# A slice of the second layer's output weights loaded by a transfer with five outer rows

## The chip, the core and the metric

The kernel runs on one core of a Trainium2 chip. The time is the device time of one execution in microseconds (us). Before the change it is 2557.82 us, the median of three runs (2560.64, 2557.49 and 2557.82). A change of 0.2% is 5.1 us.

TensorE (PE) multiplies matrices, VectorE (DVE), ScalarE (ACT) and GpSimd (POOL) work on elements, and SyncE (SP) does nothing here but issue transfers. The transfers run on the core's 16 DMA engines.

## The reference

Two layers, each an attention block over a long cache followed by a gated feed-forward block, for two batch rows of one token each (decode):

```python
x = A_x
x = x + _A_ref(_layernorm(x), A_k_cache, A_v_cache, A_wq, A_wo)   # attention, 32 query heads on 8 kv heads
x = x + _B_ref(_layernorm(x), B_w_gate, B_w_up, B_w_down)         # (gelu(x @ gate) * (x @ up)) @ down
x = x + _A_ref(...); x = x + _B_ref(...)                          # the same weights and caches again
```

The model width is 512, the cache holds 32768 positions of 128 numbers for each of 2 x 8 (batch, kv head) pairs, and everything is float32. Keys and values are 268 MB each and are read once per layer, less the little that layer 2 finds still on the chip. After attention, the 4096 numbers of the 32 heads go through `wo` (4096 x 512, 8 MB): `o @ wo`. The change is in how a part of `wo` comes on the chip in the second layer.

## The kernel before, in words

One SBUF tensor, `mem`, has 110 units of 512 float32 columns on 128 partitions. A unit is 2 KB on each partition, 256 KB in all. Every weight and cache piece has a planned place in `mem` (the function `plan`). The list `stream` holds all transfers in the order of their use: for each layer the query weights `wq`, then for each of 16 (kv head, batch) pairs keys (`kt`) and values (`vt`) in pieces of 32 units, with `wo` put in near the end, then the feed-forward weights `gu` and `wd`. The function `pump` issues the head of this list on SP as soon as the bookkeeping shows that its place has been given back by `done`; on the chip, SP then waits in this order for the semaphore of the last reader of that place. So SP's order is fixed when the program is built, and a transfer that waits holds back all that stand behind it on SP.

`wo` is loaded in two pieces in each layer (`WO_PARTS`). In layer 2, piece 0 has 28 units, the columns of heads 4 to 31, and goes to the place `A_AT = 0`, where keys stood. It is issued behind the keys of pair 14 (of 0 to 15). Its reader is `project` (L768 to L776): 28 products of one head each with one unit of `wo`, into the PSUM tile `W`. `project` stands in TensorE's loop over the pairs as a part that runs in one turn only, at pair 15:

```python
turns = [g for g, _ in ORDERS[l][1::2]][:-1]
for g in turns:
    for t in range(REP):
        pe.matmul(W[...], heads(g)[:, t, :], w[:, REP * g + t - s, :], ...)
done(("wo", l, 0))
```

In layer 2 the heads come from the top down in groups of four, so the first four products read units 24 to 27 of the 28, the last of the piece.

The end of the program is the second layer's feed-forward block. Its last weights `wd` come in pieces of 4, 3, 4, 2 and 1 units; `down` (with `add_row`, L792) multiplies them as they land, the result goes through `desk` (L935) and the transfer `out` (L936).

The helper `Program` records all operations and works out the semaphore waits. A transfer takes a semaphore of its own until it is known to have landed, and counts 16 on it. An instruction that reads what three transfers wrote waits for three semaphores.

Of the kernel before, what the change touches and what calls it, by code (L numbers as in the profile page):

```python
# [15 lines left out]
P = 128  # L16
# [3 lines left out]
DM = 512  # L20
# [36 lines left out]

WO_PARTS = [[(0, 28), (28, 4)], [(4, 28), (0, 4)]]
WO_IN = 14

LAST_ROOM = "k", 1, *ORDER[-1], 35

# [351 lines left out]
AUX = 440  # L414


def block_kernel(nc, x, kt, vt, wq, wo, gu, wd, out):
    pr = Program(nc)
    pe, dve, act, pool, sp = pr.tensor, pr.vector, pr.scalar, pr.gpsimd, pr.sync

    def sbuf(name, cols):
        return nc.alloc_sbuf_tensor(name, [P, cols], F32).ap()

    mem = sbuf("mem", UNITS * UNIT)
# [5 lines left out]
    at = {}  # L430
# [3 lines left out]
    def take(key, n):  # L434
        o = planned[key]
        if not any(s <= o and o + n <= e for s, e in holes):
            return None
        for i, (s, e) in enumerate(holes):
            if s <= o and o + n <= e:
                holes[i:i + 1] = [(x, y) for x, y in ((s, o), (o + n, e)) if y > x]  # L440
                return o
# [14 lines left out]
    def pump():  # L456
        while stream:
            key, src, cols = stream[0]
            n = cols / UNIT
            o = take(key, n)  # L460
            if o is None:
                return
            stream.popleft()
            if key == LAST_ROOM:
                held.append(ROOM_AT)
            c = int(o * UNIT)
            at[key] = (o, n), mem[:, c:c + cols]
            plain = (key[0] in "kv" and key[4] in (0, CHUNK)
                     and rolled(key[0], key[1], ORDERS[key[1]].index(key[2:4])))
            sp.dma_start(at[key][1], src, sem=(key[0], key[4]) if plain else "any")  # L470

    def flat_of(key):
        if key not in at:
            pump()
        return at[key][1]
# [4 lines left out]
    def done(key, s=0, n=None):  # L480
        o, size = at[key][0]
        n = size if n is None else n
        if s + n == size:
            del at[key]
        give(o + s, n)
        pump()

    def flat(src, g, b, s, n):
        h, c = divmod(s, CHUNK)
        return src[b, g, h, :, c * UNIT:(c + n) * UNIT]  # L490

    def add(key, src, cols):
        stream.append((key, src, cols))
# [4 lines left out]
    def rolled(kind, l, n):  # L498
        return n in ROLLED if kind == "k" else n < len(ORDER) - 1

    def add_wo(l, i):
        s, m = WO_PARTS[l][i]
        add(("wo", l, i), wo[:, s * DM:(s + m) * DM], m * DM)

    for l in range(2):
        for i, (s, m) in enumerate(pieces(WQ_SPLIT[l])):
            add(("wq", l, i), wq[:, s * DM:(s + m) * DM], m * DM)
        for n, (g, b) in enumerate(ORDERS[l]):
            for s, m in parts("k", l, (g, b)):
                add(("k", l, g, b, s), flat(kt, g, b, s, m), m * UNIT)  # L510
            if n == WO_IN:
                add_wo(l, 0)
# [24 lines left out]
    xrows = desk[:KC * NB, :P]  # L537
    act.dma_start(xrows, x)
    pump()
    ident = cst[:, C_ID:C_ID + P]  # L540
    dve.memset(ident, 0.0)
# [351 lines left out]
    def finish(l, n, p, linv):  # L893
        g, b = ORDERS[l][n]
        values(l, n, g, b, p)
        if meets(l, n)[0]:
            leave()
        combine(linv, g, b, 128 if n == len(ORDER) - 1 else 0)
# [4 lines left out]
    for l in range(2):  # L903
        queries(l)
        stage(l, 0)
        for n, (g, b) in enumerate(ORDERS[l]):
            with pr.turn_of(l, n) if n in ROLLED else nullcontext():
                if n == WO_IN + 1:
                    pr.section("project")
                    with pr.apart_of():  # L910
                        project(l)
                if n:
                    pr.section("values")
                    finish(l, n - 1, *found)
                if n == WO_IN + 1:
                    pr.section("turn")
# [21 lines left out]
    pr.emit()  # L938


_INS = ["x", "kt", "vt", "wq", "wo", "gu", "wd"]


def groups(x):
# [3 lines left out]
def halves(gate, up):  # L948
    out = []
    for e in range(2):  # L950
        c, cols = e * DF // 2, []
        for n in FW:
            cols += [gate[:, c:c + n], up[:, c:c + n]]
            c += n
        w = np.concatenate(cols, axis=1).reshape(KC, P, -1).transpose(1, 0, 2)
        out.append(np.ascontiguousarray(w).reshape(-1))
    return np.concatenate(out)


# [25 lines left out]
```

## Time and profile before

| what | value |
|---|---|
| median of three runs | 2557.82 us (2557.49 to 2560.64) |
| the profiled execution | 2558.18 us, of which the span from the first to the last instruction is 2556.7 |
| TensorE, matmul | busy 1205.1 us (47%), mean granted clock 0.738 |
| VectorE, ScalarE, GpSimd | busy 143.6, 81.3 and 2.7 us |
| data moved by the queue of SP and ACT | 1102.92 MB in 25056 packets |
| HBM read | 1102.84 MB, 431 GB/s over the span |

The page has the share of busy time by engine, the span cut into 40 equal slices (a digit is tenths of busy time), the DMA queues, and the chain of work that ended last: it is followed back from the last instruction, at each step to what released it. `DMA mem<-in_kt` there is time in which the work waited for a transfer of keys. The view of windows gives the same for stretches that one chooses, with the mean busy share of the 16 DMA engines and the GB/s that they moved. A share over 1.00 comes from packets whose recorded times overlap a little.

### The profile page before, as it was taken

The numbers are of one execution on the slowest core, as the hardware profiler recorded it, in microseconds if no ns is written. First come the engines' busy times: TensorE is split into PE (matmuls) and PEld (weight loads), VectorE is DVE, ScalarE is ACT, GpSimd is POOL, SyncE is SP. The second block draws the span as 40 slices with busy tenths as digits, with TensorE's granted clock in tenths as the row PEclk, the third lists the DMA queues.
The fourth block names the chain that finished last, engine by engine and source line by source line (L and its number), as shares of the span: only waits on it lengthen the run. The fifth ranks groups of instructions, "written<-read, shape, count | busy, mean of one in ns | idle before, by whom it ended". The sixth has DMA issues, their size and how long they took to land.

```text
span 2556.7 us, 19577 instructions
## 1 busy us (share of the span) xinstructions
PE 1205.1 (47%) x9177; PEld 317.2 (12%) x9177; DVE 143.6 (6%) x490; ACT 81.3 (3%) x190; POOL 2.7 (0%) x9
## 2 busy tenths in 40 slices
PE   3433553434544434544686444345443355343546
PEld 1100111101111111111121111111110011010112
DVE  0000000000000000000011000000000000000001
ACT  0000000000000000000010000000000000000000
POOL 0000000000000000000000000000000000000000
PEclk8766777667777767766898777677676677677778
DMA  9999999999999999999999999999999999999999
GB/s 426 428 436 430 431 438 432 438 431 437 430 431 438 432 436 432 435 429 434 427 419 436 437 431 436 431 431 438 432 438 431 436 431 431 437 433 436 433 433 386
DMA packets 25093, 1103.21 MB, mean 431 GB/s; under 512 B 2792, under 2 KB 2928, under 8 KB 5616
## 3 DMA queue, kind: packets, MB, share of 16 engines
q1 hardware_dynamic: 25056, 1102.92, 99.9%
q8 instruction: 14, 0.23, 0.0%
q14 instruction: 7, 0.06, 0.0%
q10 hardware_dynamic: 16, 0.00, 0.0%
HBM read 1102.84 MB, written 0.07 MB: 431 GB/s over the span
## 4 chain that ended last, share of the span: by engine, by line
DMA 75%; PE 23%; SPq 1%; another core or an unknown queue 0%; DVE 0%; issue 0%; ACT 0%
DMA mem<-in_kt 36%; DMA mem<-in_vt 36%; PE S L683 12%; PE A L751 11%; DMA mem<-in_wd 1%; SPq L470 1%; DMA mem<-in_gu 1%; DMA mem<-in_wq 1%; PE M L644 0%; PE A L683 0%; PE W L792 0%; ACT T L720 0%; DVE desk L722 0%; DVE aux L686 0%
## 5 line engine op out<-in xcount | busy, mean ns | idle before, releaser
L683 PE MATMUL S<-mem,aux 128*32 128x512 f32 x4032 | 543.4, 699 | 402.5 <-DMA mem<-in_kt 402.5
L751 PE MATMUL A<-mem 128*16 128x512 f32 x2048 | 292.0, 733 | 746.4 <-DMA mem<-in_vt 745.7
L683 PEld LDWEIGHTS S<-mem,aux 128*32 128x32 f32 x4032 | 137.9, 126 | 786.9 <-DMA mem<-in_kt 428.0
L751 PE MATMUL A<-mem,desk 128*16 128x512 f32 x2048 | 229.5, 601 | 12.6 <-DMA mem<-in_vt 12.6
L751 PEld LDWEIGHTS A<-mem 128*16 128x16 f32 x2048 | 61.3, 113 | 951.8 <-DMA mem<-in_vt 752.8
L686 DVE TENSOR_REDUCE aux<-S 128x1 f32<-128x512 f32 x63 | 43.6, 692 | 918.5 <-PE S L683 918.5
L766 DVE TENSOR_REDUCE aux<-M 128x4 f32<-128x64 f32 x32 | 7.2, 226 | 1334.5 <-PE M L763 1334.5
L751 PEld LDWEIGHTS A<-mem,desk 128*16 128x16 f32 x2048 | 55.3, 98 | 180.0 <-issue 167.2
L720 ACT ACTIVATE T<-S,aux 128x512 f32<-128x512 f32 x63 | 41.4, 657 | 1013.2 <-DVE aux L716 1013.2
L759 ACT ACTIVATE desk<-A,aux 128x512 f32<-128x512 f32 (+1 forms) x34 | 22.3, 662 | 1345.8 <-PE A L751 1345.8
L726 PE MATMUL M<-aux 128*128 128x4 f32 x64 | 14.6, 298 | 85.2 <-DVE aux L724 85.2
L763 PE MATMUL M<-aux,desk 128*128 128x128 f32 x128 | 21.3, 287 | 24.9 <-ACT desk L759 24.9
L644 PE MATMUL M<-mem,aux 128*32 128x512 f32 x128 | 21.2, 691 | 20.7 <-DMA mem<-in_wq 20.7
L713 PE MATMUL M<-aux 128*128 128x128 f32 x32 | 10.3, 323 | 34.5 <-DVE aux L711 34.5
L722 DVE STREAM_TRANSPOSE desk<-T 128x512 f32<-128x512 f32 x32 | 22.9, 717 | 27.0 <-ACT T L720 27.0
L726 PEld LDWEIGHTS M<-aux 128*128 128x128 f32 x64 | 11.7, 230 | 91.3 <-DVE aux L724 91.3
L722 DVE STREAM_TRANSPOSE mem<-T 128x512 f32<-128x512 f32 x32 | 22.9, 717 | 0.0
L774 PE MATMUL W<-mem,aux 128*2 128x512 f32 x112 | 17.7, 802 | 5.2 <-DMA mem<-in_wo 5.2
L763 PEld LDWEIGHTS M<-aux,desk 128*128 128x128 f32 x128 | 13.4, 141 | 53.2 <-ACT desk L759 53.2
L720 ACT ACTIVATION_READ_ACCUMULATOR T<-S,aux 128x1 f32 x63 | 12.4, 196 | 0.0
L611 PE MATMUL A<-aux 128*128 128x256 f32 (+2 forms) x38 | 12.1, 400 | 0.3 <-DVE aux L623 0.3
L713 PEld LDWEIGHTS M<-aux 128*128 128x128 f32 x32 | 4.3, 133 | 63.7 <-DVE aux L711 63.7
(108 smaller groups left out, 168.8 us busy)
## 6 DMA issues: line engine op xcount, KB each, us to landing
mem<-in_wo SPq DMA_DIRECT2D x2, 7168.0 KB
mem<-in_kt SPq DMA_DIRECT2D x2, 4096.0 KB, 16.5
mem<-in_vt SPq DMA_DIRECT2D x1, 6144.0 KB, 29.3
mem<-in_gu SPq DMA_DIRECT2D x6, 896.0 KB, 28.3
mem<-in_gu SPq DMA_DIRECT2D x3, 1792.0 KB, 40.2
mem<-in_kt SPq DMA_DIRECT2D x1, 4864.0 KB, 16.9
mem<-in_vt SPq DMA_DIRECT2D x1, 4096.0 KB, 23.8
mem<-in_vt SPq DMA_DIRECT2D x2, 2048.0 KB, 29.8
```

What stands on the lines that cost most here:

```text
L470: sp.dma_start(at[key][1], src, sem=(key[0], key[4]) if plain else "any")
L644: pe.matmul(qp[32 * t:32 * t + 32, :], window(k, v), w[:, i - s, :], start=(i < 4), stop=(i >= 8 * KC - 4))
L683: pe.matmul(banks[u][32 * t:32 * t + 32, :], pad[:, PAD_Q - 4 * c:PAD_Q + 32 - 4 * c], w[:, j - s, :], start=(j == tile_of[0]), stop=(j == ...
L686: dve.tensor_reduce(mx[:, u:u + 1], banks[u], axis=AX.X, op=OP.max)
L713: pe.transpose(m[:, :P], nm.to_broadcast([P, P]), ident)
L720: act.activation(T[u], banks[u], AF.Exp, bias=bias, scale=SCALE, accum_out=ls[:, u:u + 1])
L722: dve.transpose(p[u], T[u])
L726: pe.matmul(m[:, :REP], both.to_broadcast([P, P]), same, start=True, stop=True)
L751: pe.matmul(A[32 * t:32 * t + 16, :], p[u][:, at_p:at_p + 16], w[:, QUAD * i + t, :], start=(j == order[0]), stop=(j == order[-1]))
L759: act.activation(desk[:, i:i + 512 // n], A[:, i:i + 512 // n], AF.Copy, scale=linv)
L763: pe.transpose(m[:, c * P:(c + 1) * P], desk[:, c * P:(c + 1) * P], ident)
L774: pe.matmul(W[32 * t:32 * t + NB, :], heads(g)[:, t, :], w[:, REP * g + t - s, :], start=(g == turns[0]), stop=(g == turns[-1]))
```

## The change

The host makes a second copy of a part of `wo`, the array `wn`: of the last 768 columns of piece 0 (1.5 units, 3072 bytes on a partition) the rows of partitions 0 to 124, as five blocks of 25 rows, each with one row of zeros behind it. The zeros keep the five blocks apart in memory, so that the source of a transfer of 5 x 25 rows has an outer dimension of five. Where `pump` comes to piece 0 of layer 2, it now issues three transfers in place of one: 26.5 units on 128 partitions as before, the 1.5 units of 125 partitions from `wn`, and those of the last 3 partitions from `wo`. The place in `mem`, the readers and the order of all else are as they were. Layer 1 is not changed. The same bytes are moved.

```diff
 WO_IN = 14
+
+LANES = 5
+EACH = P // LANES
+SLIM = 768
+SLIM_AT = WO_PARTS[1][0][0] * DM + WO_PARTS[1][0][1] * DM - SLIM
...
-            sp.dma_start(at[key][1], src, sem=(key[0], key[4]) if plain else "any")
+            if key == ("wo", 1, 0):
+                slim = mem[:, c + cols - SLIM:c + cols]
+                sp.dma_start(mem[:, c:c + cols - SLIM], src[:, :cols - SLIM])
+                sp.dma_start(slim[:LANES * EACH], wn[:, :EACH])
+                sp.dma_start(slim[LANES * EACH:], src[LANES * EACH:, cols - SLIM:])
+            else:
+                sp.dma_start(at[key][1], src, sem=(key[0], key[4]) if plain else "any")
...
+def lanes(wo):
+    w = wo[:LANES * EACH, SLIM_AT:SLIM_AT + SLIM].reshape(LANES, EACH, SLIM)
+    return np.concatenate([w, np.zeros_like(w[:, :1])], axis=1)
...
+    arrays["wn"] = lanes(arrays["wo"])
```

In the built program, these rows stand on SP near the end of layer 2. A row is a line, an operation, what it writes and reads, the written shape, and the semaphores it waits for (`s_6` counts TensorE's finished instructions). Before:

```order
L470 DMA mem<-in_kt 128x16384
L470 DMA mem<-in_kt 128x16384 [waits s_6]
L470 DMA mem<-in_wo 128x14336 [waits s_6]
L470 DMA mem<-in_vt 128x16384
L470 DMA mem<-in_vt 128x16384 [waits s_6]
```

After the change, at the same place:

```order
L481 DMA mem<-in_kt 128x16384
L481 DMA mem<-in_kt 128x16384 [waits s_6]
L477 DMA mem<-in_wo 128x13568 [waits s_6]
L478 DMA mem<-in_wn 125x1x768 [waits s_6]
L479 DMA mem<-in_wo 3x768
L481 DMA mem<-in_vt 128x16384
L481 DMA mem<-in_vt 128x16384 [waits s_6]
```

Two transfers are added on SP, between the long one and the values of pair 14; the second of the three has a wait of its own, since the long one no longer covers the last 1.5 units of the old keys.

On TensorE, `project` in layer 2 is the only place that reads the piece. Before:

```order
L351 COMPARE_AND_BRANCH
L774 MATMUL W<-mem,aux 2x512 [waits s_0]
L774 MATMUL W<-mem,aux 2x512 x27
L351 UNCONDITIONAL_BRANCH
L751 MATMUL A<-mem 16x512 [waits s_9]
```

After the change:

```order
L356 COMPARE_AND_BRANCH
L785 MATMUL W<-mem,aux 2x512 [waits s_0]
L785 MATMUL W<-mem,aux 2x512
L785 MATMUL W<-mem,aux 2x512 [waits s_2,s_1]
L785 MATMUL W<-mem,aux 2x512 x25
L356 UNCONDITIONAL_BRANCH
L762 MATMUL A<-mem 16x512 [waits s_9]
```

The first product waits for the long transfer as before; the third, the first to read the last 1.5 units, waits for the two new ones.

More of the change, by code (lines that the diff above doesn't have):

```diff
@@ L414, with block_kernel @@
 AUX = 440
-def block_kernel(nc, x, kt, vt, wq, wo, gu, wd, out):
+def block_kernel(nc, x, kt, vt, wq, wo, wn, gu, wd, out):
     pr = Program(nc)
@@ L938, in block_kernel @@
     pr.emit()
-_INS = ["x", "kt", "vt", "wq", "wo", "gu", "wd"]
+_INS = ["x", "kt", "vt", "wq", "wo", "wn", "gu", "wd"]
 def groups(x):
```

## The prediction

> **What bounds the kernel now.** I read the page's slices first, then its chain of waits, then the end of the program in the views of the chain and of windows. From the page:
>
> ```profile
> span 2556.7 us, 19577 instructions
> DMA  9999999999999999999999999999999999999999
> DMA packets 25093, 1103.21 MB, mean 431 GB/s; under 512 B 2792, under 2 KB 2928, under 8 KB 5616
> q1 hardware_dynamic: 25056, 1102.92, 99.9%
> q8 instruction: 14, 0.23, 0.0%
> q14 instruction: 7, 0.06, 0.0%
> DMA 75%; PE 23%; SPq 1%; another core or an unknown queue 0%; DVE 0%; issue 0%; ACT 0%
> ```
>
> All 16 DMA engines are busy in every slice; the packets' time fills 99.9% of the span. TensorE waits for data. So the kernel is as long as its transfers, and the change moves no byte less: it can only pay in how the 16 engines share the bytes. One engine moves 431 / 16 = 26.9 GB/s. The rows q8 and q14 count 21 transfers of instructions, about 16 KB (0.23 MB / 14) and 9 KB each. They go through the same engines, in the way of the data, and nothing says that they fall evenly.
>
> Whether the engines end together is seen only where the queue runs out. The chain at the end, and stretches of half a microsecond there (columns: stretch, length, busy time and count of PE, PEld, DVE, ACT and POOL, granted clock, DMA share, GB/s):
>
> ```profile
> 2523.43 30.22 DMA mem<-in_wd
> 2553.65 0.04 issue
> 2553.69 0.62 PE W L792 x16
> 2554.31 0.02 issue
> 2554.33 0.45 PE W L792 x8
> 2554.77 0.02 issue
> 2554.80 0.29 DVE desk L935
> ```
>
> ```profile
> 2546.00:2550.00 4.00, 3.01 (x21) 0.68 (x19) 1.56 (x4) 1.46 (x3) 0.00 (x0) 1.00 1.00 412
> 2550.00:2550.50 0.50, 0.43 (x6) 0.27 (x10) 0.01 (x1) 0.00 (x0) 0.00 (x0) 1.00 0.97 389
> 2550.50:2551.00 0.50, 0.50 (x24) 0.47 (x27) 0.18 (x1) 0.00 (x0) 0.00 (x0) 1.00 0.67 270
> 2551.00:2551.50 0.50, 0.50 (x28) 0.40 (x16) 0.00 (x0) 0.00 (x0) 0.00 (x0) 1.00 0.52 209
> 2551.50:2552.00 0.50, 0.21 (x8) 0.00 (x0) 0.00 (x0) 0.00 (x0) 0.00 (x0) 1.00 0.59 217
> 2552.00:2552.50 0.50, 0.00 (x0) 0.00 (x1) 0.00 (x0) 0.00 (x0) 0.00 (x0) 1.00 0.36 143
> 2552.50:2553.00 0.50, 0.47 (x20) 0.48 (x24) 0.00 (x0) 0.00 (x0) 0.00 (x0) 1.00 0.27 102
> 2553.00:2553.50 0.50, 0.50 (x24) 0.28 (x12) 0.00 (x0) 0.00 (x0) 0.00 (x0) 1.00 0.12 45
> 2553.50:2554.00 0.50, 0.39 (x16) 0.30 (x16) 0.00 (x0) 0.00 (x0) 0.00 (x0) 1.00 0.03 12
> ```
>
> The last piece of `wd` lands at 2553.65, and from there a fixed tail of 3 us runs to the end. But the engines do not stop together. With 412 GB/s in the last full stretch, the rows of these small pieces go at 412 / 16 = 25.8 GB/s an engine. By that, 15 engines' worth of bytes move in the first half microsecond, then 10, 8, 8, 6, 4, 2, and at the end less than one. Six engines are done by about 2550.5, eight by 2551, and the last works alone until 2553.6. This bounds all that any sharing can give: from 2550 on, half the sum of the eight last rates (1387), 694 KB, is still to come; 16 engines together need 694 / 412 = 1.7 us for it and would end at 2551.7. That is 2.0 us sooner, or 0.08%. Calling 0.2% (5.1 us) what a measurement of this kernel can tell from no change, no gain of this change can be told.
>
> **The change part by part.** The long transfer of `wo` loses 1.5 units: 128 rows of 3072 bytes, 393,216 bytes, or 24,576 on each of 16 engines. At 26.9 GB/s each engine is free 0.91 us sooner.
>
> The added transfer brings 125 rows, 384,000 bytes. If its outer dimension of five means that five engines share it, each gets 25 rows, 76,800 bytes: 2.85 us at 26.9 GB/s, 2.98 at the rate of small rows. The last three rows, if on three engines, are 3072 bytes and 0.11 to 0.12 us each. Net: eleven engines are 0.91 us earlier from here to the end, two are 1.94 to 2.07 later, three 2.05 to 2.19 later.
>
> [...]
>
> The end is the last engine's end, so the sum depends on which engines the five are. If they are among the six that are done by 2550.5, they now end at 2552.6 to 2552.7, and the slowest, no longer loaded with its share, at 2553.65 - 0.91 = 2552.74: the landing is 0.9 us earlier. If the slowest is among the five, it lands at up to 2553.65 + 2.19, which is 2.2 us later. These are the bounds, -0.9 and +2.2. No row names an engine, so this is a choice: 21 instruction transfers are too few to fall evenly on 16 engines, and where one recurring cause spares six or eight of them, these are likelier neighbours (the low numbers or the high) than six picked at random. I take -0.9, by this little better than even.
>
> Issuing. Two more transfers on SP. The rows of SP around the place (start, length, what; a long one contains its waits), and the chain there:
>
> ```profile
> 2362.71 0.33 SPq L470 DMA_DIRECT2D mem<-in_kt  x1
> 2381.37 0.33 SPq L470 DMA_DIRECT2D mem<-in_wo  x1
> 2381.74 21.12 SPq L470 DMA_DIRECT2D mem<-in_vt  x2
> ```
>
> ```profile
> 2362.71 30.00 DMA mem<-in_kt
> 2392.71 0.04 issue
> ```
>
> An issue takes 0.33 us, so the two cost 0.7, perhaps twice that for the odd shape. When `wo` is issued, at 2381.37, the keys issued ahead of it are still in flight until 2392.71: 11.3 us of queued work hide this. Uncovered it would be 0.7 us on every engine. The new wait on SP, for the keys' last products, holds back the three rows and two transfers of values behind it. Those products end at about the time of the issue (the keys' readers released SP for `wo`); of the values, the first was issued at 2381.74 and the second waits 21 us anyway. Cost: nothing.
>
> TensorE. Rows around the only reader of the piece:
>
> ```profile
> 2409.69 8.90 PE L774 MATMUL W<-mem,aux 128*2 128x512 f32 x56 [2.57 <-DMA mem<-in_wo]
> 2448.39 9.19 PE L751 MATMUL A<-mem 128*16 128x512 f32 x64 [29.80 <-DMA mem<-in_vt]
> ```
>
> It already waits 2.57 us for `wo`. Later it waits 29.80 us for values. If the five make `wo` land up to 2.2 us later, this idle time takes it, and a second semaphore wait there. Behind the waiting product stand the rest of `project` and then the products with values that are not there yet, so nobody else is late. Without that cover it would be the 2.2 us once. From here on, five engines run some 3 us behind the other eleven (2.1 + 0.9). A transfer counts as landed with its last engine; the spread at the end is already about 3 us (2550.5 to 2553.6), and of the early six the five only catch up with the slow ones. So later landings do not come later. The last piece of `wd` is on its way from 2523.43, 30.22 us before it lands, so the queue holds work for engines that run ahead.
>
> Sum: 2558.18 us of the profiled execution, less 0.9 by the landing, nothing elsewhere: 2557.3. The profiled one stands 0.36 above the median of the three runs (2557.82), so 2556.9 against the median.
>
> **The rivals.**
>
> Late engines among the five. [...] Against it nothing but the grouping argument; for it, ten of 16 are not among the early six. The landing comes 1 to 2.2 us later: an engine that ends at 2552.7 goes to 2554.8, the slowest to 2555.8. Time 2559 to 2560.
>
> [...]
> [...]
>
> The transfer narrows to fewer engines: slower. If the shapes of 5 x 25 and 125 have the whole transfer put on one engine, this one has 384,000 / 26.9 = 14.3 us in place of 0.9. From 2550.5 it ends at 2563.9, the landing is 10.2 us later, and the time 2568: slower by 0.4%. It decides from two engines down: two have 7.1 us each and end at 2556.7, 3.1 us late; from one, it is over the 0.2%. The same sign would come from rows cut into many small packets. For it: nothing in the trace; against: two ordinary sizes that have five in common.
>
> It does not do what it says: all 16 engines share the 1.5 units as before. Then the skew stays and so does the time, 2557.8.
>
> **How the numbers follow.** Five early engines 0.55 (2556.9). Late engines among the five 0.22 (2559 to 2560). Ports 0.10 (2558.8). No narrowing 0.05 (2557.8). Fewer engines or small packets 0.05 (2561 to 2568). Some gain that I don't see 0.03. The four first are all inside 5.1 us of the median before: 0.92 for no difference, of which 0.01 goes to scatter of the measurement, since the three runs alone lie 3.2 us apart. Slower 0.06, faster 0.03. For the range, the first case has the scatter of the runs (-0.3 to +2.8) on it: 2556.6 to 2559.7; less another 1.6 below for a gain at the bound of 2.0 with the scatter, and above up to the second case's 2560.6: 2555.0 to 2560.6. Below and above, 2 in 10 are left.
>
> **What would show it.** The page's packets: the 125 + 3 rows of 3072 bytes add 128 to "under 8 KB" if rows stay whole, and the endings of a transfer on five and one on three engines add 8 to "under 512 B" (32 if both run on all 16; many thousands if rows are cut up). In the windows of the last 4 us, the steps tell the case. Right: 14 to 16 engines' worth longer, no stretch with one or two engines alone, and a last landing 0.9 us earlier against the end of the span. Late engines among the five: a longer stretch of four engines or fewer. [...] One engine: 10 us with 26 GB/s. At the place itself, `project` has its wait for `wo` split in two, with the sum within 2.2 us of 2.57, and the wait for values after it is shorter by what this is longer. Wrong would be any change outside the last 5 us that moves the end: a stretch of the 40 slices under 9 tenths that is at 9 now, or a later time of the last issue on SP.

## The result, and the profile after

The change makes the kernel slower: 2563.44 us, the median of 14 runs (2563.19 to 2564.16), against 2557.93 before (14 runs, 2557.49 to 2560.64). The ratio is 1.0021, with a 95% interval of 1.0013 to 1.0029. That is 5.5 us more where 0.9 us less was forecast, and outside the range.

The page's rates before (GB/s in each of the 40 slices), and then the page of the kernel after:

```profile
GB/s 426 428 436 430 431 438 432 438 431 437 430 431 438 432 436 432 435 429 434 427 419 436 437 431 436 431 431 438 432 438 431 436 431 431 437 433 436 433 433 386
```

```profile
span 2562.4 us, 19580 instructions
DMA  9999999999999999999999999999999999999998
GB/s 425 427 437 431 437 431 437 431 437 431 436 431 437 431 437 429 439 432 434 421 424 436 432 436 431 435 433 433 435 431 436 429 436 432 435 432 435 412 435 368
DMA packets 25229, 1103.21 MB, mean 431 GB/s; under 512 B 2800, under 2 KB 2936, under 8 KB 5752
```

The same bytes move and the DMA engines look as busy as before, but the third of the 40 slices from the end moves 412 GB/s where its neighbours have 435, and where the kernel before has 433. The transfer that was changed is in it. The packets answer how it was made: 8 more under 512 bytes (2800 for 2792), the endings of a transfer on five engines and of one on three, where the trace has 16 landings for a transfer of 128 rows; and 136 more under 8 KB (5752 for 5616), these 8 and the 125 + 3 rows. The semaphore events in the trace agree: the engines land the 125 rows in five steps, at 2410.00, 2410.09, 2410.44, 2411.65 and 2415.63, and the 3 rows in three, at 2410.31, 2410.40 and 2411.85. So five engines it was, with whole rows. One of them lands 4 us behind the rest, and it is none of the three that also carried a last row, which had all landed by 2411.85.

The view of windows around that transfer (columns: stretch, length, busy time and count of PE, PEld, DVE, ACT, POOL, granted clock, DMA share, GB/s), before:

```profile
2390.00:2402.00 12.00, 9.24 (x64) 2.35 (x64) 0.00 (x0) 0.00 (x0) 0.00 (x0) 0.66 1.03 444
2402.00:2416.00 14.00, 7.69 (x47) 1.82 (x43) 3.04 (x11) 1.45 (x4) 0.00 (x0) 0.63 1.00 434
2416.00:2428.00 12.00, 2.59 (x28) 0.38 (x16) 0.00 (x0) 0.00 (x0) 0.00 (x0) 0.75 1.01 437
```

and after:

```profile
2390.00:2402.00 12.00, 9.39 (x64) 2.35 (x64) 0.00 (x0) 0.00 (x0) 0.00 (x0) 0.67 0.99 430
2402.00:2416.00 14.00, 3.47 (x15) 0.84 (x15) 3.04 (x11) 1.45 (x4) 0.00 (x0) 0.60 1.01 339
2416.00:2428.00 12.00, 7.24 (x52) 1.28 (x44) 0.00 (x0) 0.00 (x0) 0.00 (x0) 0.78 1.00 431
```

In the 14 us from 2402 to 2416, the engines are as busy as ever (share 1.01) and move 339 GB/s in place of 434. A busy share says that packets are under way, not that they go at their rate. What is missing is (434 - 339) x 14 us = 1.33 MB, which is 3.1 us of all 16 engines at 431 GB/s. This is new: the forecast only shifted bytes from engine to engine. The trace also has each packet, that is, each row of a transfer on one engine. A row of 64 KB takes 2.42 us in the kernel before; here rows of that size take up to 4.10 us. All packets of this place together take 50 us longer than packets of their sizes do undisturbed, which again is 3.1 us for each of 16 engines.

TensorE around the reader of the piece, and SP at the issue:

```profile
2410.85 1.88 PE L785 MATMUL W<-mem,aux 128*2 128x512 f32 x4 [3.84 <-DMA mem<-in_wo]
2415.67 7.57 PE L785 MATMUL W<-mem,aux 128*2 128x512 f32 x52 [2.95 <-DMA mem<-in_wn]
2454.13 9.69 PE L762 MATMUL A<-mem 128*16 128x512 f32 x64 [30.89 <-DMA mem<-in_vt]
```

```profile
2381.30 0.33 SPq L477 DMA_DIRECT2D mem<-in_wo  x1
2381.67 0.94 SPq L478 DMA_DIRECT2D mem<-in_wn  x1
2382.66 0.43 SPq L479 DMA_DIRECT2D mem<-in_wo  x1
```

The wait for `wo` is 3.84 + 2.95 = 6.8 us (2.57 before). The values that TensorE waits for next land at 2454.13, where they landed at 2448.39: 5.7 us later, and this stays to the end.

The end in the chain and in windows of the kernel after:

```profile
2527.96 31.43 DMA mem<-in_wd
2559.39 0.04 issue
2559.44 0.62 PE W L803 x16
```

```profile
2552.00:2554.00 2.00, 2.00 (x19) 0.64 (x18) 0.00 (x0) 0.13 (x1) 0.00 (x0) 1.00 0.83 336
2554.00:2556.00 2.00, 1.08 (x10) 0.12 (x7) 1.30 (x4) 1.12 (x3) 0.00 (x0) 1.00 0.39 155
2556.00:2558.00 2.00, 1.64 (x42) 1.14 (x42) 0.44 (x2) 0.22 (x1) 0.00 (x0) 1.00 0.08 31
2558.00:2559.50 1.50, 1.12 (x36) 0.83 (x40) 0.00 (x0) 0.00 (x0) 0.00 (x0) 1.00 0.10 36
```

SP at the last loads, before and after:

```profile
2498.54 32.57 SPq L470 DMA_DIRECT2D mem<-in_wd  x5
```

```profile
2504.77 31.02 SPq L481 DMA_DIRECT2D mem<-in_wd  x5
```

The last landing is at 2559.39 (2553.65 before), and SP ends the issue of the last load at 2535.79 (2531.11). From 2556 on, 31 to 36 GB/s are little more than one engine. By the semaphore events, the last but one of the 16 engines lands the last piece at 2556.22, so one works alone for 3.2 us (0.7 before: 2552.99 to 2553.65). The others are later too: half of them have landed it by 2554.65, where it was 2551.43. Two losses show, then: one engine that is later than all, and a stretch in which all are slower. The experiments part them.

### The profile page after: what moved, and what is told of

Read it like the earlier page. It is cut to its first block, busy times and chain, and to the rows that moved or that the text cites. A ratio compares the mean times of both kernels' runs of the same rounds, so it can differ in the third digit from the quotient of the medians.

```text
span 2562.4 us, 19580 instructions
## 1 busy us (share of the span) xinstructions
PE 1209.0 (47%) x9177; PEld 330.6 (13%) x9177; DVE 143.6 (6%) x490; ACT 81.3 (3%) x190; POOL 2.7 (0%) x9
## 2 busy tenths in 40 slices
DMA packets 25229, 1103.21 MB, mean 431 GB/s; under 512 B 2800, under 2 KB 2936, under 8 KB 5752
## 4 chain that ended last, share of the span: by engine, by line
DMA 73%; PE 23%; another core or an unknown queue 2%; SPq 1%; DVE 0%; issue 0%; ACT 0%
DMA mem<-in_kt 37%; DMA mem<-in_vt 33%; PE S L694 12%; PE A L762 11%; DMA mem<-in_wd 2%; DMA mem<-in_wn 1%; SPq L481 1%; DMA mem<-in_gu 1%; DMA mem<-in_wq 1%; PE W L785 0%; PE M L655 0%; PE A L694 0%; PE W L803 0%; ACT T L731 0%
## 5 line engine op out<-in xcount | busy, mean ns | idle before, releaser
L694 PEld LDWEIGHTS S<-mem,aux 128*32 128x32 f32 x4032 | 150.8, 126 | 774.2 <-issue 403.8
```

The lines of the kernel that those rows point to most:

```text
L694: pe.matmul(banks[u][32 * t:32 * t + 32, :], pad[:, PAD_Q - 4 * c:PAD_Q + 32 - 4 * c], w[:, j - s, :], start=(j == tile_of[0]), stop=(j == ...
```

## The experiments

Three theories stood at the start. Theory 1: the slowest engine is one of the five, and the five write into partitions that other engines are filling, which slows both; the expectations call the way into a group of partitions a port, a word of the theory for something that no run shows. Theory 2: the slowest is one of the five, but the stretch is slow for the way `wn` lies in memory. Theory 3: the cut, with its issues and waits, costs the time. Every time below is a median of 4 to 11 runs, beside runs of the kernel before on the same chip, in which that kernel had 2557.95 to 2558.03 us.

**The cut alone.** The 1.5 units are still a transfer of their own, but of 128 rows:

```diff
-                sp.dma_start(slim[:LANES * EACH], wn[:, :EACH])
-                sp.dma_start(slim[LANES * EACH:], src[LANES * EACH:, cols - SLIM:])
+                sp.dma_start(slim, src[:, cols - SLIM:])
```

> The piece is still cut into 26.5 and 1.5 units, but the 1.5 units come as 128 rows straight from wo, so all engines share them. Theory 1 (the five engines hold the slowest one, and they write through ports that other engines are filling) and theory 2 (the five hold the slowest one, and their packets are slow for the way wn lies in memory): as before, 2557.9, within 0.5 us. Theory 3 (the cut itself, its added issue on SP and its added wait on TensorE): most of the 5.5 us stay, 2561 to 2563.4.

Measured: 2558.05 us, ratio 1.0001 (0.9992 to 1.0010). Its window, beside the 434 GB/s before and the 339 with the change:

```profile
2402.00:2416.00 14.00, 7.76 (x53) 2.30 (x57) 2.39 (x11) 1.45 (x4) 0.00 (x0) 0.76 1.03 442
```

Theory 3 is out: one more issue on SP and one more wait on TensorE cost nothing that can be told.

**The five engines, without `wn`.** The 125 rows straight from `wo`:

```diff
-                sp.dma_start(slim[:LANES * EACH], wn[:, :EACH])
+                sp.dma_start(slim[:LANES * EACH], src[:LANES * EACH, cols - SLIM:])
```

> The 125 rows on five engines, but read straight from wo, where a row follows its neighbour after 64 KB, and not from wn. Theory 1 (ports at the destination): the same as with the change, 2563.4, with packets of about 200 ns. Theory 2 (the way wn lies): packets of 121 ns, and only the imbalance is left, 2.0 us on the slowest engine, 2560.

Measured: 2563.62 us, ratio 1.0021 (1.0012 to 1.0030). Its window at the place:

```profile
2402.00:2416.00 14.00, 3.81 (x15) 0.99 (x19) 2.75 (x11) 1.45 (x4) 0.00 (x0) 0.57 1.02 352
```

The same time and the same slow stretch from another array with another layout: theory 2's cause is out. The single rows say so too: 3072 bytes take 0.12 us in the mean with the cut alone, 0.20 with the change and 0.19 here. It also shows that `wn` with its rows of zeros was not needed: the packets of this run agree with five engines for the 125 rows too, and its time is that of the change (2563.62 and 2563.44 us).

**More bytes and the place they are written to, taken apart.** If it is the partitions that cost, the same bytes on the same engines must cost more at one place than at another. So the kernel before got eight added transfers behind piece 0, which bring bytes of `wo` once more into four unused units of `mem`. Each has five rows to partitions four apart, all eight together fill partitions 0 to 19 and 32 to 51:

```diff
+            if key == ("wo", 1, 0):
+                for r in (0, 1, 2, 3, 32, 33, 34, 35):
+                    sp.dma_start(mem[r:r + 20:4, 28 * UNIT:32 * UNIT], src[r:r + 20:4, :4 * UNIT])
```

In the second kernel of the pair the destination is `mem[64 + r:64 + r + 20:4, ...]`, partitions 64 to 83 and 96 to 115, and all else is the same. By the change, where 125 rows landed in five steps and 3 in three, the eight are taken to be 64 KB more on each of five engines. The expectations call the first set the five engines' own partitions, and those that fill the second their owners. No row of a trace names an engine or a partition, so these are names for an assumption; what the pair can show is whether the place counts.

> The kernel before, with eight added transfers behind piece 0 of wo in layer 2. Each brings 5 rows of 8 KB from wo into 4 unused units of mem, to partitions r, r+4, r+8, r+12, r+16 with r = 0 to 3 and 32 to 35. [...] 64 KB more on each of five engines. Theories 1 and 2: only the engine's own time, 65.5 KB at 26.9 GB/s, 2.4 us on the slowest, 2560.3. Theory 3 (added issues): eight issues at 0.4 us, 3 us, covered by 11 us of queued work: nothing of its own.

> [...] Theory 1: the five run slower, at 17 GB/s as in the change (76.8 KB in 4.5 us) 3.8 us in place of 2.4, and the long rows beside them are held up by some 2 us as in the change: 5 to 6 us on the slowest, 2563 to 2564. Theory 2: exactly as the run with the engines' own partitions, 2560.3.

Measured: 2575.35 us (ratio 1.0068, 1.0054 to 1.0081) and 2575.79 us (1.0069, 1.0056 to 1.0083). Both missed by far, for one reason that has nothing to do with the question. The kernel's bookkeeping takes a destination's partitions as a range without steps, so it saw each transfer but the first and the fifth overlap the one before, and SP waited for that one to land. SP and the windows in the first:

```profile
2382.07 40.82 SPq L473 DMA_DIRECT2D mem<-in_wo  x8
```

```profile
2402.00:2408.00 6.00, 1.41 (x11) 0.63 (x3) 3.04 (x11) 1.45 (x4) 0.00 (x0) 0.77 0.79 340
2408.00:2424.00 16.00, 7.48 (x56) 1.41 (x56) 0.00 (x0) 0.00 (x0) 0.00 (x0) 0.82 0.07 23
```

For 16 us the queue was all but dry (share 0.07), since SP spent 40.82 us on the eight and issued nothing else; this is nearly all of the 17 us. The pair still has something to say: where hardly anything else is written, an 8 KB row takes 0.39 us to the lower partitions and 0.40 us to those 64 higher (means of the last 30 rows of each run), and the two kernels take the same time. With the bookkeeping told that the eight do not touch each other (a mark on these operations, at which `depend` skips the pair), the pair was run again.

> The eight added transfers to the five engines' own partitions again, now with the bookkeeping told that they do not touch each other (in the first version SP waited for each to land before it issued the next). 64 KB more on each of five engines, nothing else. Theories 1 (late engine and shared ports) and 2 (late engine alone): 65.5 KB at 26.9 GB/s, 2.4 us on the slowest engine: 2560.4.

> [...] Theory 1: the five share the ports and take 3.9 us (17 GB/s, as the slowest engine in the change) to 4.8 us (half rate) in place of 2.4, and the five owners are held up by 2.4 us or more: 2561.8 to 2563. Theory 2: as the run with their own partitions, 2560.4.

Measured: lower partitions 2560.32 us (ratio 1.0009, 1.0000 to 1.0018), 2.4 us more than before and just as expected. Partitions 64 higher: 2565.60 us (1.0030, 1.0018 to 1.0041), 7.6 us more and 5.3 more than its twin; theory 1's figure of at most 2563 was still too small. No run of either lies among those of the kernel before (2557.62 to 2558.51). The windows at the place, of the first and then of the second:

```profile
2402.00:2416.00 14.00, 7.33 (x51) 1.78 (x55) 2.25 (x10) 1.45 (x4) 0.00 (x0) 0.76 1.00 433
```

```profile
2402.00:2416.00 14.00, 5.15 (x31) 1.38 (x31) 3.04 (x11) 1.45 (x4) 0.00 (x0) 0.63 1.04 335
```

The same sizes and source rows, the same shape; only the written partitions differ. With the lower ones the core keeps its 433 GB/s, and 64 KB more on five engines cost 2.4 us: the time of one engine for them (65.5 KB at 26.9 GB/s), so the slowest is one of the five. With the higher ones the core falls to 335 GB/s, nearly as in the change (339). So the place counts. That an engine fills the same partitions in every transfer of 128 rows, that the lower ones are those of the five, and that it costs to write into those of others, is the reading that fits; it was not shown.

The packets of the two traces show where the rate goes. With the lower partitions no row at the place is slowed: 8 KB take 0.31 us, 64 KB take 2.42. In the twin the 8 KB rows take 0.59 us in the mean. And every long row that begins between 2405 and 2408 takes 1.7 to 2.0 times its time; at 2407 all 16 packets under way take over a tenth longer than undisturbed. With the added rows on five engines, some that carry none of them lose as well. When a single engine is left at it (from 2413 on), its 8 KB rows still take 2.1 to 2.3 times theirs and one long row 1.6 times, but nearly all other long rows 1.1 times or less. So rows to the higher partitions cost while other transfers fill these too (and next to nothing where hardly anything else is written: 0.40 us a row for 0.39 above), and more than the engines that carry them lose.

**The same rows, divided otherwise.** The whole piece, uncut by columns, as 112 and 16 partitions. The bytes and the array are those of before, in rows of the same size. The author took it that all 16 engines share both transfers, with seven rows and one row each; no view of this run counts rows by engine:

```diff
+            if key == ("wo", 1, 0):
+                sp.dma_start(at[key][1][:112], src[:112])
+                sp.dma_start(at[key][1][112:], src[112:])
+                return pump()
```

> [...] Theory 1: slower by more than 2 us, up to 15 (half rate for 17 us) though no engine has more to do. Theory 2: 2557.9, no difference.

Measured: 2581.72 us, ratio 1.0094 (1.0078 to 1.0109), 23.8 us more, beyond the 15 that was the most expected. Its windows:

```profile
2380.00:2392.00 12.00, 1.55 (x16) 0.24 (x8) 0.69 (x1) 0.00 (x0) 0.00 (x0) 0.77 1.01 352
2392.00:2404.00 12.00, 7.97 (x56) 2.08 (x60) 0.00 (x0) 0.00 (x0) 0.00 (x0) 0.66 0.99 225
2404.00:2428.00 24.00, 1.81 (x15) 0.55 (x7) 3.04 (x11) 1.45 (x4) 0.00 (x0) 0.63 1.07 195
2428.00:2440.00 12.00, 6.80 (x44) 1.37 (x48) 0.00 (x0) 0.00 (x0) 0.00 (x0) 0.60 0.84 344
```

At busy shares of 0.99 and 1.07 the core moves 195 to 225 GB/s for 36 us, half of its rate. A row of 56 KB takes 4.38 us in the mean, where it takes 2.12 in the kernel before; all packets of the place together are 374 us longer than undisturbed, or 23.4 us for each of 16 engines, as much as the kernel lost. So the rows' lower rate accounts for the loss, with no byte more and no new array: to divide 128 partitions otherwise is enough. By the reading above, the engines then write into each other's partitions; here too that was not shown. (Whether it is the place written or the place read is not told apart here; in the pair above the source rows stayed the same.)

**Half the slice.**

```diff
-SLIM = 768
+SLIM = 384
```

> The change with half the slice, 384 columns in place of 768, rows of 1536 bytes. Both theories have the loss grow with the bytes: half of 5.5, so 2560.6. If it is the count of rows that costs (125 as before, each about 80 ns slower), the loss stays near 4 to 5 us.

Measured: 2560.42 us, ratio 1.0009 (1.0000 to 1.0018), 2.5 us more, close to half of 5.5 (no run overlaps those before). The window shows it too:

```profile
2402.00:2416.00 14.00, 7.04 (x37) 1.37 (x33) 3.04 (x11) 1.45 (x4) 0.00 (x0) 0.63 1.01 393
```

(434 - 393) x 14 = 0.57 MB are missing, 1.33 with the whole slice. The loss goes with the bytes, not with the count of rows.

**Which engine is the slowest.** The run with the lower partitions again, with three and with four rows in each added transfer. In the same way these are taken to be 64 KB more on each of three engines and of four; the expectations number the engines within the five, which no row of a trace does:

```diff
-                    sp.dma_start(mem[r:r + 20:4, 28 * UNIT:32 * UNIT], src[r:r + 20:4, :4 * UNIT])
+                    sp.dma_start(mem[r:r + 12:4, 28 * UNIT:32 * UNIT], src[r:r + 12:4, :4 * UNIT])
```

> [...] In the trace of the change, the three engines that carried the last three rows were ahead of the slowest by 3 us or more. If the end is that of the slowest engine and these three run 3 us ahead of it, 2.4 us more on them cost nothing: 2557.9, within 0.5 us. If more bytes cost time wherever they go: three fifths of 2.4, 2559.4.

> [...] If the slowest is the fourth of the five, 2.4 us: 2560.3. If it is the fifth, nothing: 2557.9. Were bytes alone to cost: four fifths of 2.4, 2559.9.

Measured: three 2558.15 us (ratio 1.0001, 0.9992 to 1.0010), four 2560.39 us (1.0009, 1.0000 to 1.0019). The runs with three scatter, from 2557.84 to 2560.18, but nine of the 11 lie within 0.8 us of the median before; those with four lie at 2560.11 and above, and none before is over 2559.15. 64 KB more on each of three engines, 192 KB in all, cost nothing that the medians show: none of the three is the slowest. With four it is the 2.4 us again, all of it. So the slowest engine is one that the four rows use and the three do not, on the chip of this pair. The pair with lower and higher partitions ran on another chip, where it shows that the slowest is one of the five; in the trace of the change it is one of the two that carry no last row, since the three that do land early (by 2411.85, the slowest at 2415.63).

A version that beats both kernels does not come out of this. To relieve the slowest engine, others would have to bring its rows, and where rows were divided otherwise the core lost rate (339 GB/s in the change, 195 to 225 with 112 and 16 rows). It was not tried on that engine's rows alone.

## Why the prediction was wrong

*What bounds the kernel* held. The transfers set the time, the engines end up to 3.5 us apart (the landings of the last piece run from 2550.10 to 2553.65), and no sharing could have brought a gain that can be told. That bound spoke of gains alone; the loss has no such bound, and the text let the small size of the one stand for both.

*Five engines, and the bytes of each* held, by the packets and the landings (five steps for the 125 rows, three for the 3). The gain of 0.91 us on the other eleven does not show: in the stretch of the slice the whole core moves less, by more than these save.

*Which engines* was the choice that failed first. The five were taken to be among the six early ones, on the argument that the spared engines are neighbours; no run shows which engines are neighbours. Three rows go to engines that are not the slowest (64 KB more on them cost nothing), but a fourth row goes to the slowest of all 16, on the chip of that pair. This was the first rival, late engines among the five, at 0.22. Its price was right for what it priced: 64 KB more on an engine were worked out as 2.4 us and measured as 2.4, so the 52 KB (76.8 less 24.6) that the slice adds to the slowest engine are some 1.9 us. That is a third of the 5.5.

*The ports* have 0.10 among the chances, at 2558.8, and here lies the term that was mis-sized most. No run shows a port. What the runs showed in its place is a loss of rate that goes with the partitions written (433 GB/s for the lower, 335 for the higher). In the change the core loses 95 GB/s for 14 us, 3.1 us of all 16 engines, while the slice has 0.39 MB, which is 0.9 us of them; and in the twin of the experiments engines are slowed that carry none of the added rows. The chances also put the two cases side by side, as if only one could hold. Both losses came: 1.9 us of more bytes, and about 3.6 us left for the lower rate on the same engine (by the difference).

The packets of the engine that ends the piece last give nearly the same without a difference of medians. In the trace of the cut alone, it ends its long rows of the piece at 2408.40 and its 8 rows of the slice at 2409.38. In that of the change, its long rows end at 2410.12, 1.7 us later, and its 25 rows end at 2414.64. They take 4.52 us, where 25 at 0.124 us are 3.1: 1.4 us more. That is 3.1 us for the lower rate, and 2.1 for 17 rows more. So it stands 5.3 us behind already at the slice, and the last landing of the program is 5.7 us later than before (2559.39 for 2553.65).

*TensorE's cover* held. The wait for `wo` grew by 4.2 us, and 30.89 us of idle time before the values still followed it. What failed is the step behind it, "later landings do not come later": the values themselves landed 5.7 us later (2454.13 for 2448.39), since the same engines bring them. That step rested on the five being early and on the others losing nothing.

*SP and the cut* held: the two added issues took 0.94 and 0.43 us, about the 1.4 allowed for an odd shape, the queue covered them, and the cut alone made no difference.

*The chances.* Slower by over 0.2% had 0.06, nearly all of it on a transfer that narrows to one engine, which did not happen. Two cases that were each given less than 5.1 us passed it together, and even their highest prices on record, 2560 and 2558.8 (2.2 and 1.0 us above the median), would not have: it took the mis-sized term. The range's upper end, 2560.6, is called the second case's, but that case was priced at 2559 to 2560. Of the two signs set for a loss outside the last 5 us, the busy share did not show it (the slice stays at 9 tenths); the other did, as the last issue of a load on SP ends 4.7 us later.

## What to carry to other kernels

In this kernel a transfer of 125 rows among transfers of 128 cost several times its bytes (about 3.6 us for 0.9), and a piece in 112 and 16 rows cost 23.8 us. Where transfers follow each other without a gap, load all 128 partitions in one transfer, as the cut alone did at no cost (2558.05 us); and try added rows at more than one place (here 2.4 us at one and 7.6 us at the other). Read GB/s beside the busy share of the DMA engines; at a share of 1.07 the rate was 195 GB/s here, less than half of 431. And before bytes are moved to "early" engines, find out which these are, by adding bytes to a few and looking for no effect.

## What the runs showed of the hardware that was not expected

How the rows of a transfer are divided, and where they are written, can lower the rate of the whole core at busy shares of about 1.0: 434 GB/s fall to 339 with 125 rows on five engines, to 335 with added rows to the higher partitions (433 with the same rows to the lower), and to 195 with 112 and 16 rows. The last cost 23.8 us on a piece of 7.3 MB that takes 17 us (7.3 / 431). With the added rows to the higher partitions, every long row that began between 2405 and 2408 took 1.7 to 2.0 times its time. Added rows of 64 KB an engine cost 2.4 us at the lower partitions and 7.6 us 64 partitions higher. That engines get in each other's way at the partitions fits all of this; by what, and why engines lose that carry none of the added rows, no run here shows.

The lag of an engine stays: 64 KB more on each of four engines, some 150 us before the end, came out at the end in full (2.4 us), and as much on each of three was free. What makes one engine the slowest stays open. The 21 transfers of instructions could do it, but no run moved them.
